# Gated attention and a GELU layer: a quarter of the diagonal score block is turned from its mirror instead of computed

## The chip, the core and the metric

The kernel runs on one core of one Trainium2 chip. The metric is the device time of one execution in microseconds (us). A core has TensorE (matrix products; PE in the profile, with its weight loads as PEld), VectorE (DVE), ScalarE (ACT), GpSimd (POOL) and SyncE (SP), which here does nothing but issue transfers. Sixteen DMA engines move the data; a DMA can also turn blocks of 2-byte elements on its way, which is called a DMA transpose here.

## The reference

There are 8 sequences (batches) of 3008 rows. `z` has 64 columns, `u` and `v` have 256.

```python
scores = scale * np.matmul(z, z.transpose(0, 2, 1))     # per batch, scale = 1 / 3008
attn = np.maximum(scores, 0.0) ** 2
x = (u * np.matmul(attn, v)).reshape(24064, 256)
h = x @ w_in                                            # 256 -> 2048
g = h * (1.0 / (1.0 + np.exp(-1.702 * h)))
out = g @ w_out                                         # 2048 -> 256
```

The scores are symmetric, since both factors are `z`. Relu and square work element by element, so the squared relus are symmetric too. The scales are left out of the steps and put back at the end.

## The kernel before

**Tiles.** A batch is cut into 24 blocks of 128 rows (the last one half full) and 6 superblocks of 4 blocks, 512 rows. A *unit* n is one superblock of one batch, n = 6 * batch + `isup`, 48 in all. Unit n computes 512 rows of `attn @ v`, gates them with `u`, and hands them on as 512 rows of x. For the second layer the 24064 rows of x are cut into 47 blocks m of 512.

**Scores.** `scores(k)` (line 204) computes k pairs (n, t) in the order of the list `pairs`. A pair is two blocks, 2t and 2t+1, against the 512 columns of superblock `isup`, one block on each half of TensorE's rows (line 217). So it has 128 partitions and 2 x 512 columns. A relu (line 239 on ScalarE or line 241 on VectorE) moves it to a fp16 tile `ap_`, of which there are 20, and a square (line 228 or 230) works in place. Pairs come in bursts of three, one for each PSUM buffer.

**Symmetry between superblocks.** The list of pairs holds only t from 2 * `isup` up: blocks of the diagonal and beyond. What a unit needs of earlier superblocks is turned from the squares that an earlier unit made: `turn` (line 185) issues one DMA transpose of a whole pair tile into a tile `T`, of which there are 13. The diagonal superblock itself is computed whole: pairs t = 2 * `isup` and 2 * `isup` + 1, 4 x 4 blocks.

**Values.** `values` (line 299) adds to two PSUM banks, `O0` for the unit's first two blocks and `O1` for its last two. One matmul multiplies a 128x128 block of squares, as weights, with 256 columns of V. `squares_of` (line 276) says which tile holds the block, `squares_at` (line 283) when the planner takes it to be ready, and `drop` (line 288) counts uses. `halves` (line 335) does the half block 23 of a batch on 64 rows. When a unit ends, VectorE multiplies the banks by `u` into `X` (line 322) and `turn_x` (line 251) turns X by DMA into a ring `XT`.

**Second layer.** `hidden` (line 355) makes 1024 hidden columns in a PSUM tile `hg`, ScalarE the sigmoid (line 362), VectorE the product GT (line 366), and `outs` (line 391) adds up the result, which leaves through `ysb` (lines 400, 402) and a store (line 407). The work of block m = n - 2 is laid between that of unit n.

**The order of the work.** All engines run lists that a planner writes when the program is built. The planner keeps a clock for each engine (`now`) and costs of each kind of operation (`cost`). The main loop walks the list `work` of value, hidden and output steps in a fixed order and puts a burst of scores in where three PSUM buffers are free and fewer than 20 squares are held; so scores run ahead of their use. `push` gives a relu, a square or an exit to whichever of ScalarE and VectorE ends it sooner. `send` gives transfers to SyncE, by due unit. Whatever the plan, SyncE then works through its list strictly in order, and a transfer whose data or target is not ready holds back all behind it. Real waits are semaphores that follow from the tiles. The first V, z and W loads are issued by GpSimd; its later loads are triggered by a tiny copy of the newest squares (`hold`).

```python
for n in range(NU + 1):
    m = n - 2
    ...
            work.append(("r", n, [NJ - 1]))
            work.append(("o", n, list(range(NJ - 7, NJ - 1)), 0, True))
```

Of the kernel before, what the change touches and what calls it, by code (L numbers as in the profile page):

```python
# [9 lines left out]
F16 = mybir.dt.float16  # L10
P = 128
# [3 lines left out]
def kernel(  # L15
# [10 lines left out]
    AF = mybir.ActivationFunctionType  # L26
    ALU = mybir.AluOpType

    B, S, D = u.shape
    DQK = z.shape[2]  # L30
# [4 lines left out]
    ISUP = 512  # L35
    NIB = ISUP // P
    NIS = (S + ISUP - 1) // ISUP
# [10 lines left out]
    CSC = 16.0  # L48
    FSC = CSC * CSC * float(S) * float(S)

    dve, act, pe, sp, pool = nc.vector, nc.scalar, nc.tensor, nc.sync, nc.gpsimd
# [8 lines left out]
    ptp = ctx.enter_context(tc.tile_pool(name="ptp", bufs=1))  # L60
# [44 lines left out]
    def turn_z(b):  # L105
# [7 lines left out]
    T_SC, T_SW, T_MM, T_HG = 0.215, 0.1, 0.109, 0.215  # L113
    T_LAT, T_SEM, T_DMA = 0.25, 0.1, 3.5
# [1 line left out]
    cost = {  # L116
        ("act", "relu"): 1.03, ("dve", "relu"): 1.23, ("act", "sq"): 1.03, ("dve", "sq"): 0.7,
        ("act", "out"): 0.6, ("dve", "out"): 0.7, ("act", "sig"): 1.03, ("dve", "gt"): 1.23, ("dve", "gate"): 0.7,
        ("sp", "turn"): 1.45, ("sp", "turn_x"): 2.6, ("sp", "store"): 0.6,
    }  # L120
    BOTH = ("act", "dve")
    ops = []
# [4 lines left out]
    def push(ready, kind, engines, fn):  # L127
        ops.append((ready, len(ops), kind, engines, fn))
        ops.sort(key=lambda o: o[0])

    def send(ready, kind, due, fn, ok=None):
        sends.append((ready, kind, due, fn, ok))
# [17 lines left out]
    def pe_at(rows_, dur):  # L150
        if mode[0] != rows_:
            now["pe"] += T_SW
            mode[0] = rows_
        now["pe"] += dur
        return now["pe"] + T_LAT
# [3 lines left out]
    A, A_at, a_left = {}, {}, {}  # L159
# [6 lines left out]
    def take_ps():  # L166
        nonlocal ps_next
        i = ps_next % 3
        ps_next += 1
        ps_free[i] = None  # L170
        return i

    latest = [None]
# [5 lines left out]
    def set_ps(i, at):  # L179
        ps_free[i] = at  # L180
# [4 lines left out]
    def turn(n, t, at):  # L185

        b, isup = divmod(n, NIS)
        key = (b * NIS + t // 2, isup)
        if key not in T:
            c = colors.pop(0)  # L190
            T_col[key] = c
            T[key] = ptp.tile([P, NIB, NIB, P], F16, name=f"T{c}", tag=f"T{c}")
            T_left[key] = [2, NIB]
        a = A[(n, t)]
        g0 = (t % 2) * 2
        sp.dma_start_transpose(
            T[key][:, g0:g0 + 2, :, :].rearrange("p g i r -> p (g i) r"), a.rearrange("p g c -> p (g c)"),
        )
        T_left[key][0] -= 1
        if T_left[key][0] == 0:  # L200
            T_at[key] = at + T_DMA
        a_left[(n, t)] -= 1

    def scores(k):

        nonlocal nxt
        for i in range(k):
            n, t = pairs[nxt]
            nxt += 1
            b, isup = divmod(n, NIS)  # L210
            Z = ZT[b % 2]
            assert b in turned
            p_ = take_ps()
            sc = psA.tile([P, 2, ISUP], F32, name="sc", tag="A")
            for g in range(2):
                h0 = g * DQK
                pe.matmul(  # L217
                    sc[:, g, :], Z[h0:h0 + DQK, 2 * t + g, :],
                    Z[h0:h0 + DQK, isup * NIB:(isup + 1) * NIB, :],
                    start=True, stop=True,  # L220
                )
            a = pap.tile([P, 2, ISUP], F16, name="ap_", tag="ap_")
            A[(n, t)] = a
            a_left[(n, t)] = 2 + (t // 2 > isup)

            def squared(e, at, n=n, t=t, a=a, isup=isup):
                if e == "act":
                    act.activation(a, a, AF.Square, scale=1.0)
                else:
                    dve.tensor_tensor(a, a, a, ALU.mult)  # L230
                A_at[(n, t)] = at
                latest[0] = a
                if t // 2 > isup:
                    key = (n - isup + t // 2, isup)
                    send(at, "turn", key[0], lambda at: turn(n, t, at), lambda: key in T or len(colors) > 0)

            def relu(e, at, p_=p_, sc=sc, a=a, squared=squared):
                if e == "act":
                    act.activation(a, sc, AF.Relu, scale=CSC)  # L239
                else:  # L240
                    dve.tensor_scalar(a, sc, 0.0, CSC, ALU.max, ALU.mult)  # L241
                set_ps(p_, at)
                push(at, "sq", BOTH, squared)

            push(pe_at(DQK, T_SC), "relu", BOTH, relu)

    Os, Ys, GTs, Xs, ysbs = {}, {}, {}, {}, {}
    stored = set()
# [27 lines left out]
    def squares_of(n, j, ib):  # L276

        J = j // NIB
        if J < n % NIS:
            return T[(n, J)][:, ib, j % NIB, :]  # L280
        return A[(n, j // 2)][:, j % 2, ib * P:(ib + 1) * P]

    def squares_at(n, j):

        J = j // NIB
        return T_at.get((n, J)) if J < n % NIS else A_at.get((n, j // 2))

    def drop(n, j):
        J = j // NIB
        if J < n % NIS:  # L290
            key = (n, J)
            T_left[key][1] -= 1
            if T_left[key][1] == 0:
                colors.append(T_col.pop(key))
                del T[key], T_left[key], T_at[key]
        else:
            a_left[(n, j // 2)] -= 1

    def values(n, js, h, ends):
# [6 lines left out]
        for j in js:  # L306
            for i2 in range(2):
                ib = 2 * h + i2
                pe.matmul(  # L309
                    O[:, i2, :], squares_of(n, j, ib), V[:, j, :],  # L310
                    start=(j == 0 and i2 == 0), stop=(ends and j == js[-1] and i2 == 1),
                )
# [22 lines left out]
    def halves(n):  # L335

        V = V16[n // NIS % 2]
        for q in range(NIB // 2):
            for h in range(2):
                lo, ib = h * SREM, 2 * h + q  # L340
                pe.matmul(  # L341
                    Os[(n, h)][:, q, :], squares_of(n, NJ - 1, ib)[lo:lo + SREM, :], V[lo:lo + SREM, NJ - 1, :],
                    start=False, stop=False,
                )
        pe_at(DQK, 2 * T_MM)
        drop(n, NJ - 1)
# [150 lines left out]
    keep_q(0)  # L497
    cast_z(2)
    scores(3)
    keep_q(1)  # L500
    turn_q(2)
# [7 lines left out]
    def ready_of(w):  # L509

        if w[0] in "or":
            at = [squares_at(w[1], j) for j in w[2]] + ([bank[w[3]]] if w[0] == "o" and w[2][0] == 0 else [])
        elif w[0] == "h":
            at = xt_at[w[1] * TB // 64:(w[1] + 1) * TB // 64] + [ps_free[ps_next % 3]]
        else:
            at = [GTs.get((w[1], w[2]), (None, None))[1]] + ([bank[h] for h in w[3]] if w[2] == 0 else [])
        return None if None in at else max(at)
# [13 lines left out]
    while wi < len(work):  # L531
# [15 lines left out]
        if burst:  # L547
            now["pe"] = max([now["pe"]] + ps[:k])
            scores(k)
            n = w[1]  # L550
            ahead = squares_at(n, NJ - 1)
            if w[2][0] >= EDGE and n not in halved and ahead is not None and ahead <= now["pe"]:
                halves(n)
                halved.add(n)
            continue
# [54 lines left out]
```

## Time and profile before

| what | value |
|---|---|
| median of 3 runs | 1274.05 us (1271.99 to 1276.13) |
| the profiled execution | 1274.22 us |
| its span, first to last instruction | 1272.5 us |
| mean granted TensorE clock | 0.995 |
| TensorE busy | 99%, 9824 matmuls |
| VectorE, ScalarE busy | 66%, 59% |
| SyncE's transfers (queue q1) | 381600 packets, 130.87 MB, 52.5% of the DMA engines' span |
| score matmuls (line 217) | 672 of 64x512, 93.1 us |
| value matmuls (line 309) on T tiles | 1920 of 128x256, 229.5 us |

A line of the profile's groups gives source line, engine, operation, output and inputs, count, then busy time and the mean in nanoseconds of one, then the idle time of the engine in front of them and what ended it. A line of a timeline gives start, length, engine, line, operation and count, and in brackets the idle time ahead with its releaser. "SPq" is SyncE issuing a transfer; the time to its landing is listed with the DMA issues. Busy time of TensorE includes the tail of each pipelined matmul, so a row of matmuls advances by less than the mean of one.

### The profile page before, as it was taken

How to read it: one execution, taken by the hardware profiler on the slowest of the kernel's cores; microseconds unless marked ns; L12 is line 12 of the kernel's file. 1: busy time of each engine (PE TensorE's matmuls, PEld its weight loads, DVE VectorE, ACT ScalarE, POOL GpSimd, SP SyncE). 2: the span in 40 equal slices, each digit the busy share in tenths (PEclk: the TensorE clock that was granted, in tenths of full speed). 3: DMA queues.
4: the chain of work that ended last, by engine and by line, in shares of the span. 5: the costliest groups of instructions: out<-in, count | busy, mean ns of one | idle time of the engine just before them, and what ended most of it. 6: DMA issues, size and time to landing. Idle time of an engine off the chain costs nothing.

```text
span 1272.5 us, 23287 instructions
## 1 busy us (share of the span) xinstructions
PE 1256.7 (99%) x9824; PEld 901.3 (71%) x9824; DVE 834.7 (66%) x864; ACT 749.8 (59%) x765; POOL 80.9 (6%) x130
## 2 busy tenths in 40 slices
PE   8999999999999999999999999999999999999998
PEld 4667677777777777777777777777777777777775
DVE  6477776666676666766567665776657766677446
ACT  6466776555665556655566565665656655566234
POOL 2101001010000100001000010000100001000000
PEclk8899999999999999999999999999999999999999
DMA  9997569673587745867457684667856678454201
GB/s 190 185 194 130 120 120 152 108 133 93 111 141 118 125 100 113 130 121 133 96 106 130 118 134 106 103 123 119 142 99 112 132 110 142 87 104 87 74 26 41
DMA packets 431225, 149.80 MB, mean 118 GB/s; under 512 B 356112, under 2 KB 430864, under 8 KB 431120
## 3 DMA queue, kind: packets, MB, share of 16 engines
q1 hardware_dynamic: 381600, 130.87, 52.5%
q0 software_dynamic: 49520, 17.44, 13.8%
q8 instruction: 77, 1.26, 0.4%
q14 instruction: 28, 0.23, 0.1%
HBM read 60.29 MB, written 24.64 MB: 67 GB/s over the span
## 4 chain that ended last, share of the span: by engine, by line
PE 97%; DMA 2%; ACT 1%; DVE 0%; SPq 0%; issue 0%; DVEq 0%; ACTq 0%
PE O L309 38%; PE yps L391 26%; PE hg L355 25%; PE sc L217 6%; PE O L341 1%; DMA T<-ap__359 1%; DMA zst<-in_z_dram 1%; ACT ysb L400 0%; DMA T<-ap__266 0%; SPq L81 0%; DVE X L322 0%; DVE GT L366 0%; DVE ap__363 L241 0%; ACT tsg L362 0%; ACT ap__154 L239 0%
## 5 line engine op out<-in xcount | busy, mean ns | idle before, releaser
L366 DVE TENSOR_TENSOR GT<-hg,tsg 128x1024 f16<-128x1024 f32 x376 | 460.2, 1225 | 339.8 <-ACT tsg L362 336.2
L362 ACT ACTIVATE tsg<-hg 128x1024 f16<-128x1024 f32 x376 | 384.8, 1024 | 389.3 <-PE hg L355 389.3
L355 PE MATMUL hg<-XT,W 128*128 128x512 f16 x1504 | 385.6, 379 | 0.6 <-DVE GT L366 0.6
L391 PE MATMUL yps<-W,GT 128*128 128x256 f16 x3008 | 366.8, 273 | 0.0
L391 PEld LDWEIGHTS <-GT 128*128 128x128 f16 x3008 | 293.9, 98 | 84.7
L309 PE MATMUL O<-V,T 128*128 128x256 f16 x1920 | 229.5, 274 | 3.5 <-DMA T<-ap__317 2.5
L309 PEld LDWEIGHTS <-T 128*128 128x128 f16 x1920 | 182.8, 98 | 55.4 <-issue 24.5
L355 PEld LDWEIGHTS <-W 128*128 128x128 f16 x1504 | 147.2, 98 | 98.7 <-issue 0.9
L217 PE MATMUL sc<-ZT 64*128 64x512 f16 x672 | 93.1, 382 | 0.4 <-ACT ap__154 L239 0.3
L400 ACT ACTIVATE ysb<-yps 128x512 f32<-128x512 f32 x47 | 28.1, 597 | 95.5 <-PE yps L391 95.5
L402 DVE TENSOR_SCALAR ysb<-yps 128x512 f32<-128x512 f32 x47 | 32.5, 692 | 57.0 <-PE yps L391 57.0
L322 DVE TENSOR_TENSOR X<-O,RU 128x512 f16<-128x512 f32 x96 | 65.4, 681 | 0.5 <-PE O L309 0.4
L217 PEld LDWEIGHTS <-ZT 64*128 64x128 f16 x672 | 23.8, 94 | 37.8 <-issue 24.2
L81 POOL DMA_DIRECT2D V<-in_v_dram x32 | 27.3, 855 | 5.2 <-issue 3.7
L101 POOL COPY z<-z 128x1536 f16<-128x1536 f16 x7 | 10.3, 1465 | 52.1 <-DMA z<-in_z_dram 52.1
L81 POOL DMA_DIRECT2D z<-in_z_dram x7 | 10.6, 1513 | 1.1 <-issue 0.8
L87 POOL DMA_DIRECT2D V<-in_v_dram x16 | 9.0, 571 | 0.0
L87 POOL DMA_DIRECT2D z<-in_z_dram x14 | 7.6, 553 | 0.0
L488 PE MATMUL ztp<-ident,z 128*128 128x128 f16 x24 | 2.8, 290 | 4.2 <-ACT z L483 4.2
L483 ACT ACTIVATE z<-zst 128x384 f16<-128x384 f32 x4 | 2.1, 523 | 7.6 <-DMA zst<-in_z_dram 7.6
L482 DVE CAST z<-zst 128x384 f16<-128x384 f32 x4 | 1.4, 360 | 7.4 <-DMA zst<-in_z_dram 7.4
L488 PEld LDWEIGHTS <-z 128*128 128x128 f16 x24 | 2.2, 132 | 5.4 <-ACT z L483 5.1
(1499 smaller groups left out, 1322.0 us busy)
## 6 DMA issues: line engine op xcount, KB each, us to landing
out_dram<-ysb SPq DMA_DIRECT2D x94, 256.0 KB, 2.4
RU<-in_u_dram SPq DMA_DIRECT2D x40, 512.0 KB, 4.1
V<-in_v_dram POOLq DMA_DIRECT2D x24, 384.0 KB, 7.6
RU<-in_u_dram SPq DMA_DIRECT2D x8, 384.0 KB, 3.7
z<-in_z_dram POOLq DMA_DIRECT2D x7, 368.0 KB, 9.1
V<-in_v_dram POOLq DMA_DIRECT2D x8, 320.0 KB, 8.2
XT<-X SPq DMA_TRANSPOSE x144, 2.4
W<-in_moe_w_in_dram POOLq DMA_DIRECT2D x1, 1024.0 KB, 10.4
```

The source lines that it names most:

```text
L81: eng.dma_start(dst[:, :full - lo, :], dram[b, lo * P:full * P].rearrange("(n p) d -> p n d", p=P),)
L87: eng.dma_start(dst[h * SREM:(h + 1) * SREM, NF - lo, :], dram[b, NF * P:S].unsqueeze(1))
L217: pe.matmul(sc[:, g, :], Z[h0:h0 + DQK, 2 * t + g, :], Z[h0:h0 + DQK, isup * NIB:(isup + 1) * NIB, :], start=True, stop=True,)
L309: pe.matmul(O[:, i2, :], squares_of(n, j, ib), V[:, j, :], start=(j == 0 and i2 == 0), stop=(ends and j == js[-1] and i2 == 1),)
L322: dve.tensor_tensor(Xs[n][:, :, 2 * h:2 * h + 2, :].rearrange("p c n d -> p n c d"), Os.pop((n, h)).rearrange("p n (c d) -> p n c d", c=NK ...
L341: pe.matmul(Os[(n, h)][:, q, :], squares_of(n, NJ - 1, ib)[lo:lo + SREM, :], V[lo:lo + SREM, NJ - 1, :], start=False, stop=False,)
L355: pe.matmul(hg[:, e, :], W1[:, k, ff * P:(ff + 1) * P], XT[:, k, p0:p0 + TB], start=(k == 0), stop=(k == NK - 1),)
L362: act.activation(tsg, hg, AF.Sigmoid, scale=1.702 / FSC)
L366: dve.tensor_tensor(GT, hg, tsg, ALU.mult)
L391: pe.matmul(Ys[h][:, i2, :], GT[:, e, s * P:(s + 1) * P], W2[:, ff, :], start=(ff == 0 and i2 == 0), stop=(ff == NFF - 1 and i2 == 1),)
L400: act.activation(o, y, AF.Copy, scale=1.0 / FSC)
L402: dve.tensor_scalar(o, y, 1.0 / FSC, None, ALU.mult)
```

## The change

For every unit from n = 2 on, the second diagonal pair, t = 2 * `isup` + 1, is computed only in its right half: the matmuls, the relu and the square work on 256 of 512 columns. The missing quarter of the diagonal superblock, blocks 2 and 3 against blocks 0 and 1, is the mirror of the right half of the first diagonal pair. `turn_diag` turns it with two DMA transposes of 128x256 on SyncE into a tile `Dt`, which has three buffers. The value matmuls of `O0` for those two blocks read `Dt`; those of `O1` read the half pair as before. The planner gets costs for the half operations and for the new transfers (`diag`), sends them with the unit as due time, and takes both `Dt` and the half pair to be needed before the value step of such a block.

```diff
@@ -116,7 +116,9 @@
-        ("sp", "turn"): 1.45, ("sp", "turn_x"): 2.6, ("sp", "store"): 0.6,
+        ("sp", "turn"): 1.45, ("sp", "diag"): 2.4,
+        ("act", "relu_half"): 0.6, ("dve", "relu_half"): 0.7, ("act", "sq_half"): 0.6, ("dve", "sq_half"): 0.45,
+        ("sp", "turn_x"): 2.6, ("sp", "store"): 0.6,
@@ -201,6 +203,17 @@
+    Ds, D_at = {}, {}
+
+    def turn_diag(n, at):
+
+        t = n % NIS * 2
+        Ds[n] = ptp.tile([P, 2, 2, P], F16, name="Dt", tag="Dt", bufs=3)
+        for g in range(2):
+            sp.dma_start_transpose(Ds[n][:, g, :, :], A[(n, t)][:, g, 2 * P:])
+        D_at[n] = at + T_DMA
+        a_left[(n, t)] -= 1
+
@@ -212,37 +225,43 @@
+            low = 2 if n >= 2 and t == 2 * isup + 1 else 0
             for g in range(2):
                 h0 = g * DQK
                 pe.matmul(
-                    sc[:, g, :], Z[h0:h0 + DQK, 2 * t + g, :],
-                    Z[h0:h0 + DQK, isup * NIB:(isup + 1) * NIB, :],
+                    sc[:, g, low * P:], Z[h0:h0 + DQK, 2 * t + g, :],
+                    Z[h0:h0 + DQK, isup * NIB + low:(isup + 1) * NIB, :],
                     start=True, stop=True,
                 )
...
-            a_left[(n, t)] = 2 + (t // 2 > isup)
+            a_left[(n, t)] = 2 + (t // 2 > isup or (n >= 2 and t == 2 * isup))
+            half = "_half" if low else ""
+            cols = slice(low * P, ISUP)
...
+                elif n >= 2 and t == 2 * isup:
+                    send(at, "diag", n, lambda at: turn_diag(n, at))
...
-            push(pe_at(DQK, T_SC), "relu", BOTH, relu)
+            push(pe_at(DQK, T_SC / 2 if low else T_SC), "relu" + half, BOTH, relu)
@@ -278,11 +297,15 @@
+        if n >= 2 and J == n % NIS and j % NIB >= 2 and ib < 2:
+            return Ds[n][:, ib, j % NIB - 2, :]
         return A[(n, j // 2)][:, j % 2, ib * P:(ib + 1) * P]
 
     def squares_at(n, j):
 
         J = j // NIB
+        if n >= 2 and J == n % NIS and j % NIB >= 2:
+            return max(D_at[n], A_at[(n, j // 2)]) if n in D_at and (n, j // 2) in A_at else None
```

In between, the relu and the square take `cols` of their tiles in place of whole tiles, under the costs with `half` in their names.

More of the change, by code (lines that the diff above doesn't have):

```diff
@@ L223, in scores, with squared @@
             A[(n, t)] = a
-            a_left[(n, t)] = 2 + (t // 2 > isup)
-            def squared(e, at, n=n, t=t, a=a, isup=isup):
+            a_left[(n, t)] = 2 + (t // 2 > isup or (n >= 2 and t == 2 * isup))
+            half = "_half" if low else ""
+            cols = slice(low * P, ISUP)
+            def squared(e, at, n=n, t=t, a=a, isup=isup, cols=cols):
+                s_ = a[:, :, cols]
                 if e == "act":
-                    act.activation(a, a, AF.Square, scale=1.0)
+                    act.activation(s_, s_, AF.Square, scale=1.0)
                 else:
-                    dve.tensor_tensor(a, a, a, ALU.mult)
+                    dve.tensor_tensor(s_, s_, s_, ALU.mult)
                 A_at[(n, t)] = at
-                latest[0] = a
+                latest[0] = a[:, :, cols]
                 if t // 2 > isup:
@@ L235, in squared, with relu @@
                     send(at, "turn", key[0], lambda at: turn(n, t, at), lambda: key in T or len(colors) > 0)
-            def relu(e, at, p_=p_, sc=sc, a=a, squared=squared):
+                elif n >= 2 and t == 2 * isup:
+                    send(at, "diag", n, lambda at: turn_diag(n, at))
+            def relu(e, at, p_=p_, sc=sc, a=a, squared=squared, half=half, cols=cols):
                 if e == "act":
-                    act.activation(a, sc, AF.Relu, scale=CSC)
+                    act.activation(a[:, :, cols], sc[:, :, cols], AF.Relu, scale=CSC)
                 else:
-                    dve.tensor_scalar(a, sc, 0.0, CSC, ALU.max, ALU.mult)
+                    dve.tensor_scalar(a[:, :, cols], sc[:, :, cols], 0.0, CSC, ALU.max, ALU.mult)
                 set_ps(p_, at)
-                push(at, "sq", BOTH, squared)
-            push(pe_at(DQK, T_SC), "relu", BOTH, relu)
+                push(at, "sq" + half, BOTH, squared)
+            push(pe_at(DQK, T_SC / 2 if low else T_SC), "relu" + half, BOTH, relu)
     Os, Ys, GTs, Xs, ysbs = {}, {}, {}, {}, {}
```

## The prediction

> **What bounds the kernel now.** I read the page first: TensorE is busy in 99% of the span, and the costliest groups show it waiting for nothing but a few microseconds of transposes.
>
> ```profile
> span 1272.5 us, 23287 instructions
> PE 1256.7 (99%) x9824; PEld 901.3 (71%) x9824; DVE 834.7 (66%) x864; ACT 749.8 (59%) x765; POOL 80.9 (6%) x130
> PEclk8899999999999999999999999999999999999999
> DMA  9997569673587745867457684667856678454201
> L309 PE MATMUL O<-V,T 128*128 128x256 f16 x1920 | 229.5, 274 | 3.5 <-DMA T<-ap__317 2.5
> L217 PE MATMUL sc<-ZT 64*128 64x512 f16 x672 | 93.1, 382 | 0.4 <-ACT ap__154 L239 0.3
> ```
>
> So a matmul saved is time saved, and a wait put before a matmul is time lost, since nothing later has idle time to give back. The same page shows a weak place: in the first slices the DMA engines are 90% busy and the clock below full. I therefore asked for the timeline of TensorE and the clock table there (columns: stretch, length, busy time of PE, PEld, DVE, ACT, POOL with counts, granted clock, DMA share, GB/s).
>
> ```profile
> 43.76 1.94 PE L309 MATMUL O<-V,T 128*128 128x256 f16 x15
> 48.16 0.61 PE L309 MATMUL O<-V,T 128*128 128x256 f16 x2 [2.46 <-DMA T<-ap__317]
> ...
> 44.20:47.60 3.40, 1.50 (x13) 0.97 (x10) 0.19 (x1) 0.59 (x1) 0.00 (x0) 1.00 2.43 129
> 47.60:51.00 3.40, 2.66 (x12) 1.62 (x13) 0.00 (x0) 0.00 (x0) 1.58 (x2) 0.50 1.18 283
> 51.00:54.40 3.40, 3.40 (x18) 2.40 (x16) 0.00 (x0) 0.00 (x0) 0.00 (x0) 0.50 1.18 240
> 54.40:57.90 3.50, 3.50 (x30) 2.71 (x29) 0.00 (x0) 0.62 (x1) 0.00 (x0) 0.99 1.33 131
> ```
>
> A wait of 2.46 us for a transpose was followed by about 6.8 us at clock 0.50. A late transpose costs its wait and a slow stretch after it.
>
> Last, the SyncE queue and TensorE around unit 3 (its squares are ap__844 and later):
>
> ```profile
> 76.89 2.54 SPq L264 DMA_TRANSPOSE XT<-X  x2
> 79.49 0.57 SPq L81 DMA_DIRECT2D RU<-in_u_dram  x1
> 80.16 0.96 SPq L407 DMA_DIRECT2D out_dram<-ysb  x2
> 81.22 3.31 SPq L196 DMA_TRANSPOSE T<-ap__852  x1
> ...
> 74.13 0.82 PE L217 MATMUL sc<-ZT 64*128 64x512 f16 x6
> 81.85 1.04 PE L309 MATMUL O<-V,ap__844 128*128 128x256 f16 x8
> 82.72 0.60 PE L309 MATMUL O<-V,ap__848 128*128 128x256 f16 x4
> ...
> T<-ap__852 SPq DMA_TRANSPOSE x1, 8.4
> ```
>
> The queue runs without a gap from 36.6 to 81.2 us, each entry starting as the one before ends, so whatever is put into it there moves everything behind it. The transpose issued at 81.22 took 8.4 us to land, at 89.6.
>
> **The change part by part.**
>
> *Score matmuls.* 46 of 336 pairs (units 2 to 47) go from 512 to 256 columns. The burst of three pairs takes 0.82 us for six matmuls with the last one's 0.38 in it: (0.82 - 0.38)/2 = 0.22 a pair. The nearest row for a 256-column pair on half the rows is L341, four matmuls in 0.38 with a last one of 0.27: 0.11 a pair. Saved: 46 x 0.11 = 5.0 us. Lower end: if the pair's two weight loads (94 ns each, L217 PEld) ran one behind the other, a pair could not go under 0.19, and 1.4 us is saved; L341 has the same 64-row loads and gets 0.11, so I take 5.0. The issue order of the changed kernel has as many bursts (118) and the same number of value matmuls (4416); 78 of 9824 places differ, by a few places each, so no mode switch is added.
>
> *Relu and square.* The 92 half operations are cheaper (0.60 against 1.02 on ScalarE and 0.69 against 1.23 on VectorE, by the 128x512 and 128x1024 rows). In the new order 29 operations go from ScalarE to VectorE; summed by those rows VectorE's share of this work falls from 302 to 294 us and ScalarE's from 348 to 307. Both engines are off the path (66% and 59% busy): 0. What covers it is the time by which score bursts run ahead; if that were gone, a late PSUM buffer would hold TensorE directly, but the work shrinks.
>
> *Diagonal transposes, units 4 to 47.* Each unit adds two issues on SyncE (nearest rows: XT pieces, 1.22 us whatever their size), so 2.4 us a unit, 92 x 1.22 = 112 us in all on a queue with room, and 64 KB a piece of DMA. Counting matmuls times their rows between the score burst and the first value matmul that reads the mirror: 34 and 30 us in units 4 and 5, 52 to 79 us from unit 6 on. Transit is some 2.6 us to the issue (burst 338.65, transpose issued 341.26), 2.4 of issues and at most the 9.4 us that I found as a landing in mid-kernel. Nothing waits: 0.
>
> *The ring of three mirror tiles.* SyncE must wait for the last read of unit n-3. By the order this is met early but for the first unit of each batch from batch 2 on (n = 12, 18, ... 42). At n = 18: burst at 392.12, the mirror of unit 15 last read by the matmuls on ap__3987 at 401.4. SyncE stands until about 401.6, issues the mirror until 404.1, four T transposes (8.2 us by their rows of before, 395.61 to 404.4) until 412.3, then XT, which lands near 417.4. Queued behind it are also a load and two stores with more room. The first hidden matmul on that XT is at 426.39: 9 us of cover, cost 0. With cover gone it is paid six times (a rival below).
>
> *Unit 2.* Its mirror is issued behind T from ap__363, at 49.1 and 50.3, and moves T from ap__367 and all behind it 2.4 us later. Neighbours land after 4.6, 4.2 and 3.3 us, small XT pieces after 2.4: the second piece lands at 52.7 to 54.9. TensorE reads it at 53.6, in the slow stretch. Cost 0 to 1.3, I take 0: the row above it in time landed at 52.4, and these pieces are a quarter of it.
>
> *Unit 3.* Its mirror stands in SyncE's order right behind the two stores, in the place of the transpose of 81.22, but 2.4 us later because of unit 2's mirror: issued at 83.6 and 84.8. TensorE wants it at 82.5 (the matmuls on ap__848 at 82.72, less the two shortened pairs that come after the wait of 2.46 us). So TensorE waits, with its hidden and output matmuls queued behind. Bounds: without the 2.4 us shift, and by the fastest XT (2.5 us, 1.2 us after 81.2), it lands at 84.9: 2.4 us. With the whole shift and the 8.4 us: 93.2, 10.7 us. (The whole shift and the fastest XT give 87.3, 4.8 us.) The nearest row is the one whose place it takes: landing at 89.6, later by part of the 2.4, sooner because the two pieces hold half its bytes. I take 89.6: 7.1 us lost.
>
> *The clock after that wait.* The one wait of 2.46 us gave some 6.8 us at 0.50. A slow stretch of that length, all of it worked through, loses half of it, 3.4 us; one of half the length loses 1.7, and since part of it can fall into the wait itself I take 2.6, the middle. Ends 0 (the wait ends before the clock falls) and 3.4.
>
> The Trainium skill, TensorE: Matmul & The Clock Gate, section Why this matters for your kernels, wants no idle gap beyond about 3 us, since one idle window brings the half rate back, and its Part 1 lets a single busy window of about 3.4 us restore it. The trace loses the clock already at 2.46 us of waiting and takes two such lengths to regain it. By the page's return this term would be 1.7 and the sum 1278.0.
>
> Sum: -5.0 + 0 + 0 + 0 + 0 + 7.1 + 2.6 = +4.7 us. The profiled execution took 1274.2 us (span 1272.5 and 1.7 around it), the median of the runs 1274.05, so 1278.9 us.
>
> **The rivals.**
>
> A. *The forecast*: one long wait in unit 3 and its slow clock eat the gain. Own range, by the bounds with unit 2's: from 1274.2 - 5.0 + 4.8 + 1.7 = 1275.7 to 1274.2 - 5.0 + 10.7 + 3.4 + 1.3 = 1284.6.
>
> B. *Unit 3's mirror comes in time; faster*. SyncE's entries of over 1.3 us (2.14, 2.40, 2.52) show it held up by full transfers, not by issuing, and small pieces may slip in. Then the whole 5.0 stays: 1269.2. It decides if the second piece lands by 83.6, 1.1 us after it is wanted. Against: even the fastest landing with no shift is 84.9. With a wait of 2.4 us and no slow clock it would be 1271.6.
>
> C. *The ring of three blocks SyncE until XT is late*, in six batches: past 9 us of extra lateness each further 3 us costs 6 x (3 + 2.6) = 34 us, 1312 with A's. For it: V loads in those stretches stretch landings to 9.4 us. Against: the cover worked out above.
>
> D. *The change does not do what it says*: the halved pair is bound by its weight loads, only 1.4 us saved, and A's wait stays: 1274.2 - 1.4 + 9.7 = 1282.5. Against it stands L341.
>
> **How the numbers follow.** Chances: A 0.72, B 0.12, C 0.06, D 0.10. About 0.3%, 3.8 us, is what a measurement of this kernel can tell from no change. A's sum stands just past it: I give 0.45 of its 0.72 to slower, 0.27 to the same, since shift, landing and clock may each fall short by 2 us. Faster is B, 0.12; slower 0.45 + 0.06 + 0.10 = 0.61; same 0.27. The range takes A and D whole and reaches halfway into B, down to 1270; its top is A's, 1285. Left out are C and about half of B.
>
> **What would show it.** Score matmuls with 256 columns, 92 of them, at 0.11 a pair; an idle entry of 4 to 10 us before the value matmul on Dt in unit 3, released by that DMA, and clock 0.50 behind it; no such entry in unit 2 over 1.3 us; SyncE waiting on TensorE near 400 us with no idle TensorE after it; from 100 us to the end a stretch shorter by about 4.7 us. I would be wrong if the SyncE queue drains earlier than 81 us, if the mirror overtakes the stores, or if TensorE is already later than 82.5 there.

## The result, and the profile after

The changed kernel takes 1279.75 us (median of 7 runs, 1277.44 to 1283.44), the kernel before 1273.96 us (7 runs, 1271.99 to 1276.13). The ratio is 1.0046 with a 95% interval of 1.0031 to 1.0062: slower by some 6 us. The profiled execution of the changed kernel took 1279.29 us, 5.1 more than that of before.

The page of the changed kernel, its head and the groups that answer to those shown of before (line 332 was 309, line 231 was 217):

```profile
span 1277.2 us, 23484 instructions
PE 1251.8 (98%) x9824; PEld 900.8 (71%) x9824; DVE 826.5 (65%) x893; ACT 707.8 (55%) x736; POOL 81.9 (6%) x130
...
PEclk8989999999999999999999999999999999999999
DMA  9997659694497945979458774696747767554201
...
L332 PE MATMUL O<-V,T 128*128 128x256 f16 x1920 | 229.0, 274 | 4.4 <-DMA T<-ap__359 3.4
...
L231 PE MATMUL sc<-ZT 64*128 64x512 f16 (+1 forms) x672 | 88.0, 367 | 0.7 <-ACT ap__154 L258 0.3
...
L332 PE MATMUL O<-V,Dt 128*128 128x256 f16 x168 | 31.3, 275 | 8.4 <-DMA Dt<-ap__847 8.4
```

TensorE does less: 1251.8 us of busy time for 1256.7, and the score matmuls alone give 5.1 (93.1 to 88.0). And yet the span is longer by 4.7 us. The last line holds the reason: value matmuls on the new tile `Dt` were preceded by 8.4 us of idleness, all of it ended by one transfer, the mirror made from ap__847. That is unit 3's.

The timelines of SyncE and of TensorE around that place, changed kernel:

```profile
78.41 2.84 SPq L283 DMA_TRANSPOSE XT<-X  x2
81.30 0.57 SPq L81 DMA_DIRECT2D RU<-in_u_dram  x1
81.97 0.96 SPq L430 DMA_DIRECT2D out_dram<-ysb  x2
83.03 3.91 SPq L213 DMA_TRANSPOSE Dt<-ap__847  x2
...
81.33 1.04 PE L332 MATMUL O<-V,ap__847 128*128 128x256 f16 x8
90.80 0.76 PE L332 MATMUL O<-V,Dt 128*128 128x256 f16 x2 [8.44 <-DMA Dt<-ap__847]
```

SyncE has no gap ahead of the mirror: it was held by its queue, not by its data, for the squares of ap__847 were done at 75.99 and the mirror was issued 7.0 us later. SyncE's entries stand some 1.8 us later than before (the load of `u` at 81.30 for 79.49). TensorE was ready at 82.36 (90.80 less 8.44).

The clock around the wait (stretch, length, busy PE, PEld, DVE, ACT, POOL, granted clock, DMA share, GB/s):

```profile
82.00:86.00 4.00, 0.36 (x4) 0.08 (x1) 0.00 (x0) 0.26 (x1) 0.83 (x1) 1.00 1.29 243
86.00:90.00 4.00, 0.00 (x0) 0.00 (x0) 0.00 (x0) 0.00 (x0) 0.00 (x0) 0.61 1.35 248
90.00:94.00 4.00, 3.20 (x12) 1.54 (x13) 0.00 (x0) 0.27 (x1) 0.00 (x0) 0.53 1.12 215
94.00:98.00 4.00, 4.00 (x31) 2.47 (x30) 2.62 (x3) 1.78 (x2) 0.00 (x0) 1.00 0.56 107
```

The clock falls while TensorE idles. It stays at half until about 93.7, if it takes no value but 1.00 and 0.50: then 0.53 over the four us from 90 is half clock for 0.47/0.50 of them. So some 3 us of work ran at half speed.

Three landmarks close the account. These are the last value matmuls ahead of the wait, the first score burst behind unit 3's work and the last output matmuls, first of the kernel before, then of the changed one:

```profile
81.85 1.04 PE L309 MATMUL O<-V,ap__844 128*128 128x256 f16 x8
101.07 0.82 PE L217 MATMUL sc<-ZT 64*128 64x512 f16 x6
1264.46 3.66 PE L391 MATMUL yps<-W,GT 128*128 128x256 f16 x32
```

```profile
110.66 0.71 PE L231 MATMUL sc<-ZT 64*128 64x512 f16 x6
1269.48 3.66 PE L414 MATMUL yps<-W,GT 128*128 128x256 f16 x32
```

With 81.33 for the first (shown above) the changed kernel is 0.5 us ahead, then 9.6 behind, then 5.0 behind. So 10.1 us were lost inside unit 3, 8.4 of them idle and the rest by the clock, and 4.6 us were won back by the 43 half pairs that are computed from that burst on (units 5 to 47), 0.106 us each.

### The profile page after: what moved, and what is told of

The parts are those of the page before. It is cut to its first block, busy times and chain, and to the rows that moved or that the text cites. A ratio compares the mean times of both kernels' runs of the same rounds, so it can differ in the third digit from the quotient of the medians.

```text
span 1277.2 us, 23484 instructions
## 1 busy us (share of the span) xinstructions
PE 1251.8 (98%) x9824; PEld 900.8 (71%) x9824; DVE 826.5 (65%) x893; ACT 707.8 (55%) x736; POOL 81.9 (6%) x130
## 4 chain that ended last, share of the span: by engine, by line
PE 94%; DMA 3%; SPq 1%; ACT 1%; DVE 1%; issue 0%; DVEq 0%; ACTq 0%
PE O L332 38%; PE hg L378 25%; PE yps L414 24%; PE sc L231 6%; PE O L364 1%; DMA T<-ap__359 1%; DMA Dt<-ap__847 1%; DMA RU<-in_u_dram 1%; DMA zst<-in_z_dram 1%; SPq L283 0%; ACT ysb L423 0%; SPq L290 0%; DMA T<-ap__266 0%; DVE X L345 0%; SPq L81 0%
## 5 line engine op out<-in xcount | busy, mean ns | idle before, releaser
L231 PE MATMUL sc<-ZT 64*128 64x512 f16 (+1 forms) x672 | 88.0, 367 | 0.7 <-ACT ap__154 L258 0.3
L332 PE MATMUL O<-V,Dt 128*128 128x256 f16 x168 | 31.3, 275 | 8.4 <-DMA Dt<-ap__847 8.4
L332 PEld LDWEIGHTS <-Dt 128*128 128x128 f16 x168 | 16.1, 98 | 14.0 <-DMA Dt<-ap__847 9.0
```

Of the source, the lines that this page charges most:

```text
L231: pe.matmul(sc[:, g, low * P:], Z[h0:h0 + DQK, 2 * t + g, :], Z[h0:h0 + DQK, isup * NIB + low:(isup + 1) * NIB, :], start=True, stop=True,)
L332: pe.matmul(O[:, i2, :], squares_of(n, j, ib), V[:, j, :], start=(j == 0 and i2 == 0), stop=(ends and j == js[-1] and i2 == 1),)
```

## The experiments

The theory: unit 3's mirror is late because it stands behind a full SyncE queue, this wait and its slow clock are the whole loss, and each unit gains 0.11 us. The rival: the price is spread, by the traffic and the SyncE time of 92 transposes, or the halved pairs save less than thought. The edits are against the changed kernel. Each ratio is to runs of the kernel before that were taken beside the experiment; their medians lie between 1272.97 and 1274.13 us.

**The mirror from unit 4 on.**

```diff
-            low = 2 if n >= 2 and t == 2 * isup + 1 else 0
+            low = 2 if n >= 4 and t == 2 * isup + 1 else 0
```

and the same in the other four places where `n >= 2` stands.

> The mirror is used from unit 4 on instead of unit 2. Theory (one late mirror: unit 3's transposes stand at the end of a SyncE queue that has no gap, the wait of 8.4 us and the slow clock behind it are the whole loss, and each of the other units gains 0.11 us): no idle entry on a Dt tile, 44 x 0.11 = 4.8 us saved, 1274.0 - 4.8 = 1269.2 us. Rival (the loss is spread: the transposes cost a little in every unit by their traffic and their time on SyncE, and the halved pairs save less than 5 us): 44/46 of the loss stays, about 1279 us.

Measured: 1269.47 us, ratio to before 0.9963 (0.9948 to 0.9977). The loss is gone and the gain is there. No value matmul of the trace waits for a `Dt`. Two units of 46 decided between slower and faster, and the spread price is refuted.

**The mirror in unit 3 alone.**

```diff
-            low = 2 if n >= 2 and t == 2 * isup + 1 else 0
+            low = 2 if n == 3 and t == 2 * isup + 1 else 0
```

and the same in the other four places.

> The mirror is used in unit 3 alone. Theory (one late mirror): nearly the whole loss without the gain. Two forms of it: if SyncE's order sets the landing, the absence of unit 2's two issues brings it 2.4 us earlier, the wait is 6.0 us and the time 1274.0 + 6.0 + 1.6 (clock) - 0.1 = 1281.5 us; if the transfers ahead of it set the landing (V load, u load, two stores), the wait stays near 8 us and the time is about 1283.5 us. Rival (the loss is spread over the units): one unit in 46 changes nothing that can be seen, 1274.1 us.

Measured: 1282.15 us, 1.0063 (1.0045 to 1.0081), so one unit costs 8.7 us by the medians and 5.7 to 10.3 by the interval. Both forms of the theory lie inside it, so the trace has to tell them apart. In the waits of its trace the tile made from ap__844 is unit 3's mirror (engine, line, releaser, us in total, times, longest):

```profile
PE O L332 <- DMA Dt<-ap__844: 5.0, 2, 4.6
```

Without unit 2's two issues SyncE issued the mirror at 80.95 and not at 83.03, and the first gap, up to the first matmul on the mirror, is 4.6 us for 8.4. Of these 3.8 us, 2.1 are the earlier issue, 0.9 a faster landing of the piece that this matmul waits for (6.8 us after its issue for 7.7), and 0.8 TensorE's later arrival (the matmuls on ap__844 at 82.14, those on ap__847 at 81.33). So SyncE's order is the larger part of what changed, and not all of it. TensorE came later because of a wait near 46 us that both kernels have, 3.3 us long here and 2.5 in the profile of before. By the landmarks this execution lost 7.1 us inside unit 3 (82.14 to 108.50, before 81.85 to 101.07), 5.0 of them idle, and its whole span is longer by 7.3.

**Mirrors turned, but not used.** The second pair is computed whole, and `squares_of` gives it to the value matmuls.

```diff
-                    sc[:, g, low * P:], Z[h0:h0 + DQK, 2 * t + g, :],
-                    Z[h0:h0 + DQK, isup * NIB + low:(isup + 1) * NIB, :],
+                    sc[:, g, :], Z[h0:h0 + DQK, 2 * t + g, :],
+                    Z[h0:h0 + DQK, isup * NIB:(isup + 1) * NIB, :],
...
-            cols = slice(low * P, ISUP)
+            cols = slice(0, ISUP)
...
-        if n >= 2 and J == n % NIS and j % NIB >= 2 and ib < 2:
-            return Ds[n][:, ib, j % NIB - 2, :]
```

> All mirrors are turned into Dt, but the second diagonal pair is computed whole as before and the value matmuls read it, so nothing reads Dt. Theory (one late mirror): 92 transposes more on SyncE and in the DMA engines cost nothing by themselves, 1274.0 us within 1.5. Rival (the loss is spread): the traffic and SyncE's time are the price, 1278 us or more.

Measured: 1273.82 us, 0.9997 (0.9986 to 1.0008). 92 transposes cost nothing that can be resolved, at most 1.0 us by the interval, as long as nobody waits for them.

**Half pairs without a mirror.** This kernel leaves out the mirrored quarter of the diagonal; a block of the first diagonal pair is read in its place.

```diff
-        Ds[n] = ptp.tile([P, 2, 2, P], F16, name="Dt", tag="Dt", bufs=3)
-        for g in range(2):
-            sp.dma_start_transpose(Ds[n][:, g, :, :], A[(n, t)][:, g, 2 * P:])
...
-            return Ds[n][:, ib, j % NIB - 2, :]
+            return A[(n, 2 * J)][:, j % 2, ib * P:(ib + 1) * P]
```

> The second diagonal pair is computed in its right half, and where the mirror would be read a block of the first diagonal pair is read, so no mirror is turned and that quarter of the diagonal is wrong in the output. Theory (one late mirror, each half pair saves 0.11 us): 1274.0 - 46 x 0.11 = 1269.0 us. Rival (a half pair is bound by its weight loads, 0.19 us): 1274.0 - 1.4 = 1272.6 us.

Measured: 1269.14 us, 0.9961 (0.9950 to 0.9973), a saving of 3.4 to 6.4 us. The bound by weight loads (1.4 us) lies outside. The page of the changed kernel agrees when the shapes of its score matmuls are kept apart:

```profile
L231 PE MATMUL sc<-ZT 64*128 64x512 f16 x580 | 86.3, 383 | 0.7 <-ACT ap__154 L258 0.3 <-DVE ZT L514 0.2 <-ACT ap__146 L258 0.2
L231 PE MATMUL sc<-ZT 64*128 64x256 f16 x92 | 12.5, 269 | 0.0
```

A single one takes 269 ns for 383, 0.11 us less, and a pair runs side by side on the two halves of the rows.

**Unit 2, without unit 3.**

```diff
-            low = 2 if n >= 2 and t == 2 * isup + 1 else 0
+            low = 2 if n >= 2 and n != 3 and t == 2 * isup + 1 else 0
```

and the same in the other four places.

> The mirror is used in unit 2 and from unit 4 on, not in unit 3. Theory (unit 3's mirror alone is late, unit 2's costs nothing): 1273.7 - 45 x 0.11 = 1268.8 us, as without unit 2 within the noise. Rival (unit 2's mirror is late as well, or its two issues push something else into lateness): an idle entry on Dt in unit 2, and 1271 us or more.

Measured: 1270.12 us, 0.9972 (0.9957 to 0.9987), within the noise of the kernel that begins at unit 4. It lies between the two forecasts and does not decide. But its profiled execution (1272.24 us) shows the entry that the rival names (a timeline of TensorE, then the clock table):

```profile
51.46 1.04 PE L332 MATMUL O<-V,ap__441 128*128 128x256 f16 x8
55.27 0.70 PE L332 MATMUL O<-V,Dt 128*128 128x256 f16 x2 [2.77 <-DMA Dt<-ap__441]
...
48.00:51.00 3.00, 1.47 (x12) 1.10 (x13) 0.00 (x0) 0.00 (x0) 1.58 (x2) 1.00 1.02 185
51.00:55.00 4.00, 1.49 (x14) 1.09 (x12) 0.00 (x0) 0.00 (x0) 0.00 (x0) 1.00 0.91 229
55.00:58.00 3.00, 2.73 (x13) 1.87 (x14) 0.00 (x0) 0.00 (x0) 0.00 (x0) 0.50 1.30 135
```

Unit 2's mirror was late by 2.77 us here. In the profiled execution of the changed kernel the same read came at 53.72 and waited for nothing. There the clock had fallen earlier, after the wait near 46 us that is in both, so TensorE reached the read later. Here the clock was still full and TensorE was there at 52.50 (55.27 less 2.77), 1.2 us earlier, while SyncE issued the mirror 2.0 us later (51.84 for 49.83). So unit 2's mirror is not free in every execution; a shift of some 2 us in SyncE's queue or in TensorE's work decides. The timing does not resolve its price: 1270.12 and 1269.47 differ by less than the width of either interval.

**Six mirror tiles instead of three.**

```diff
-        Ds[n] = ptp.tile([P, 2, 2, P], F16, name="Dt", tag="Dt", bufs=3)
+        Ds[n] = ptp.tile([P, 2, 2, P], F16, name="Dt", tag="Dt", bufs=6)
```

> The changed kernel with six Dt buffers instead of three, so that SyncE no longer stands and waits for the last read of unit n-3 at the start of each batch. Theory (9 us of cover hide that standstill): 1279.7 us as before within 1.5. Rival (the standstill costs in six batches): 1276 us or less.

Measured: 1281.20 us, 1.0056 (1.0042 to 1.0070), the same as the changed kernel. SyncE's timelines, first of the changed kernel, then with six tiles, around unit 18's mirror, which with three tiles has to wait for unit 15's last read:

```profile
409.89 2.46 SPq L213 DMA_TRANSPOSE Dt<-ap__4577  x2
417.94 2.53 SPq L283 DMA_TRANSPOSE XT<-X  x2
```

```profile
402.44 2.47 SPq L213 DMA_TRANSPOSE Dt<-ap__4577  x2
416.40 2.50 SPq L283 DMA_TRANSPOSE XT<-X  x2
```

The standstill is real: the mirror leaves 7.5 us later. But XT behind it leaves only 1.5 us later. Its second piece is issued at 419.2 and lands 2.5 us later, near 421.7, and the hidden matmuls that read it begin at 434.49. The cover is some 13 us.

**Filling the wait with work.** 38 matmuls of 512 columns into a free PSUM buffer, used for nothing, right before unit 3's first read of its mirror.

```diff
+        if n == 3 and h == 0 and js[0] == 4 * (n % NIS) + 2:
+            p_ = take_ps()
+            fill = psA.tile([P, 2, TB], F32, name="fill", tag="A")
+            for _ in range(38):
+                pe.matmul(fill[:, 0, :], W1[:, 0, :P], W1[:, 1, :TB], start=True, stop=True)
+            set_ps(p_, now["pe"])
```

> The changed kernel with 38 score-sized matmuls without use (8.2 us of work at full clock) put right before unit 3's first read of its mirror, into a free PSUM buffer. They fit into the wait of 8.4 us and keep TensorE working through it. Theory (idleness brings the slow clock, which costs 1.6 us after the wait): the clock stays at 1.00 from 82 to 98 us and the time falls to 1278.1 us. Rival (the slow clock has another cause, or costs nothing): 1279.7 us, and if the filling is longer than the wait, more.

Measured: 1277.97 us, 1.0033 (1.0018 to 1.0048). The trace shows what was expected (the timeline, then the clock table):

```profile
81.77 8.36 PE L333 MATMUL fill<-W 128*128 128x512 f16 x38
90.50 0.59 PE L338 MATMUL O<-V,Dt 128*128 128x256 f16 x2 [0.37 <-DMA Dt<-ap__847]
...
86.00:90.00 4.00, 4.00 (x20) 1.67 (x17) 0.00 (x0) 0.00 (x0) 0.00 (x0) 1.00 1.29 246
90.00:94.00 4.00, 3.61 (x25) 1.99 (x24) 0.74 (x1) 1.08 (x2) 0.00 (x0) 1.00 1.22 171
```

The mirror lands as late as ever, TensorE is busy all the while, and the clock stays at 1.00. That the idleness brought the slow clock here is shown by this. Its price, 1.8 us by the medians, is as forecast, but the intervals of the two kernels overlap. The traces show it more closely: from the last value matmuls ahead of the wait to the first score burst behind unit 3's work it is 28.2 us with the filling (80.89 to 109.05) and 29.3 without (81.33 to 110.66).

**Batch 1's V loads one unit later.**

```diff
-            at(n0 + 3 + q // 2, 3 + 9 * (q % 2), lambda b=b, q=q: load_v(b, q))
+            at(n0 + (4 if b == 1 else 3) + q // 2, 3 + 9 * (q % 2), lambda b=b, q=q: load_v(b, q))
```

> The changed kernel with the four loads of V for batch 1 one unit later, so that GpSimd issues none of them while unit 3's mirror is on its way. Theory (the mirror is late by SyncE's full queue, and beyond that by the load that shares the DMA engines): the two pieces land 2.4 to 4 us after their issue instead of 5.4 and 7.7, the wait shrinks from 8.4 to about 5 us, and the time is about 1276 us. Rival (SyncE's order alone decides): wait and time as in the changed kernel, 1279.7 us.

Measured: 1275.69 us, 1.0015 (1.0001 to 1.0029), clear of the changed kernel. Its wait in unit 3, and the transfers of that time (name, count, size, median us from issue to landing), first of the changed kernel, then of this one:

```profile
Dt<-ap__847 SPq DMA_TRANSPOSE x2, 6.6
V<-in_v_dram POOLq DMA_DIRECT2D x1, 384.0 KB, 8.8
```

```profile
PE O L332 <- DMA Dt<-ap__847: 3.4, 1, 3.4
...
Dt<-ap__847 SPq DMA_TRANSPOSE x2, 3.6
```

The pieces land after 3.6 us for 6.6 and the wait falls from 8.4 to 3.4 us. Of the 5.0 us, 3.5 are a faster landing of the piece that the first matmul waits for (4.2 us after its issue for 7.7), 1.1 the earlier issue (81.95 for 83.03), and 0.4 TensorE's later arrival (the matmuls on ap__847 at 81.75 for 81.33). So the load that GpSimd had in flight on the same DMA engines held 3.5 us of the wait, and part of the earlier issue may be its doing too, since the transfers ahead shared the engines with it. That the rest is SyncE's full queue is argued from the issue 7.0 us behind the data and from the kernel with unit 3 alone; a mirror put further ahead in SyncE's list was not tried. The time falls by 4 and not by 5 us: more of the slow stretch now falls on work (86.22 to about 91.9).

**A version that beats both.** The wait near 46 us that both kernels have looks like the same thing: transposes of a full SyncE queue beside a GpSimd load, there of z. The kernel with the mirror from unit 4 on, and that load, with its turning, three quarters of a unit later in the planned order:

```diff
-        at(n0 + 1, 12, lambda b=b: load_z(b))
-        at(n0 + 2, 12, lambda b=b: turn_z(b))
+        at(n0 + (2 if b == 1 else 1), 6 if b == 1 else 12, lambda b=b: load_z(b))
+        at(n0 + (3 if b == 1 else 2), 6 if b == 1 else 12, lambda b=b: turn_z(b))
```

> The mirror from unit 4 on, and the load of z for batch 1 (GpSimd) with its turning one unit later than before, so that no GpSimd load shares the DMA engines with the transposes that unit 2 waits for near 46 us. Theory (a transpose is late where a GpSimd load shares the engines with a full SyncE queue, and the slow clock follows): the wait of 3.8 us near 46 us and most of its 6.8 us at clock 0.50 go, 1269.5 - 3.8 - 2.9 = 1262.8 us. Rival (those transposes are late by SyncE's own queue): 1269.5 us.

Measured: 1264.11 us (1263.89 to 1264.52), 0.9923 (0.9901 to 0.9944) of before. The timelines of TensorE, first with the mirror from unit 4 alone, then with the later load:

```profile
49.84 3.17 PE L332 MATMUL O<-V,T 128*128 128x256 f16 x14 [3.63 <-DMA T<-ap__359]
```

```profile
43.71 3.94 PE L332 MATMUL O<-V,T 128*128 128x256 f16 x32
47.49 1.04 PE L332 MATMUL O<-V,ap__441 128*128 128x256 f16 x8
```

All 32 value matmuls on T tiles now run without a break, the clock is 1.00 from 40 to 64 us, and no wait of TensorE for a transpose is left. The transposes that were late before show why (median us to landing), first with the mirror from unit 4 alone, then with the later load:

```profile
T<-ap__317 SPq DMA_TRANSPOSE x1, 6.1
T<-ap__359 SPq DMA_TRANSPOSE x1, 8.7
```

```profile
T<-ap__317 SPq DMA_TRANSPOSE x1, 3.4
T<-ap__359 SPq DMA_TRANSPOSE x1, 3.3
```

They are issued within 0.5 us of the same times (39.69 and 41.06, then 39.22 and 40.60), so the rival, SyncE's own queue, is refuted here. In the trace the load starts only 3.9 us later (43.44 for 39.51). Beside it now stand the transposes from ap__363 and ap__367, which land after 10.5 and 10.0 us, and nobody waits for them.

## Why the prediction was right

The forecast was 1278.9 us with slower as its likeliest case; 1279.75 was measured, and the mechanism was the one named. Two terms were mis-sized in opposite directions, so part of the closeness is luck. Step by step:

- *Score matmuls, 5.0 us saved.* Right. 3.4 to 6.4 by the half pairs without a mirror, and 0.106 us a unit by the landmarks, 4.9 for 46.
- *Relu and square, nothing.* Right. VectorE's busy time fell from 834.7 to 826.5 us and ScalarE's from 749.8 to 707.8; I had -8 and -41.
- *Transposes of units 4 to 47, nothing.* Right, by the mirrors turned but not used, and by the mirror from unit 4 on. Late landings come there too, 7.4 us for the mirror made from ap__9485, and nobody waits.
- *The ring of three, nothing.* Right; the standstill is there, and the cover was 13 us where I had 9, since the four T transposes ahead of XT took 5.4 us and not 8.2.
- *Unit 2, 0 of 0 to 1.3.* Right for the profiled execution of the changed kernel, mis-sized as a bound: 2.77 us in another kernel's execution. I had placed the mirror's issue and TensorE's arrival by one execution, whose clock was slow at that moment, and took both for fixed.
- *Unit 3, 7.1 us.* The mechanism was right, the size 8.4. I took the landing of the transpose in whose place the mirror stands, 89.6; the first value matmul on it began at 90.80. SyncE issued it at 83.03, 0.6 us sooner than forecast. The row I took, 8.4 us from issue to landing, had a load of V by GpSimd beside it (issued at 83.15), so that load was in the sum without my naming it; without it the piece that counts landed 3.5 us sooner.
- *The clock, 2.6 us.* Some 1.7 by the landmarks (10.1 lost, 8.4 of it idle). About 6.8 us at half clock came as expected, but some 3.9 of them fell into the longer wait and so cost nothing, where the 2.6 left room for 1.6 there. The two errors of size, +1.3 and -0.9, nearly cancel, and that is luck.

The faster rival failed at its own condition: the mirror would have had to land by 83.6. The rival that the halved pair saves little is refuted, and so is the ring.

## What to carry to other kernels

A change that pays in every unit can be lost in one: where TensorE has no idle time, look at the first units, in which queues are full and work does not yet run ahead, before summing the gain. Ask of each new transfer what stands in front of it on its queue, what other queue loads the DMA engines at that moment, and when its reader arrives; then begin the change behind the tight units. A wait is worth its length and the slow clock behind it, and the profile of the kernel before shows both if it is asked for the one stretch where they already happen.

## What was not expected

- The mirror's 64 KB transposes land in 2.4 us in the median, the shortest in 2.3 and the longest in 8.1; unit 3's, beside a 384 KB load of another queue and behind two stores, took 5.4 and 7.7. Moving loads that TensorE did not wait for was worth 4 us in one place and 5 us in another.
- How long the clock stays low varies: after the wait near 46 us about 6.8 us in the profile of before, but in that of the changed kernel only part of this:

```profile
47.60:51.00 3.40, 1.05 (x6) 0.75 (x7) 0.00 (x0) 0.00 (x0) 0.63 (x1) 0.76 1.56 209
51.00:54.40 3.40, 3.40 (x25) 2.74 (x24) 0.00 (x0) 0.00 (x0) 0.95 (x2) 0.74 0.91 206
54.40:57.90 3.50, 3.50 (x30) 2.65 (x28) 0.00 (x0) 0.93 (x1) 0.00 (x0) 1.00 1.18 156
```

If the clock takes no value but 1.00 and 0.50, a granted clock of 0.76 is half clock for (1 - 0.76)/0.5 = 48% of the stretch, 0.74 for 52%: 3.4 us in all, half the other length. The traces suggest what decides. In the first 3.4 us at half clock TensorE was busy for 2.82 us in the changed kernel and for 3.11 without unit 3, and the full clock came back; it was busy for 2.69 us in the kernel before, 2.14 in unit 3 with the later V loads and 2.03 with the mirror from unit 4 on, and the clock stayed low for as long again. No experiment tried this.
- The version with no wait for a transpose also scatters least: 6 runs within 0.6 us, where 7 runs of the changed kernel spread over 6.0 and the 35 of the kernel before in one session over 8.2. That the scatter comes from the early waits and the clock behind them is a guess.
